# The first segment of a two-layer memory attention + GeGLU kernel in two units of 256 queries, with joined exponentials and a new instruction order

## The chip, the cores and the metric

The kernel runs on one core of one Trainium2 chip. TensorE (PE) multiplies, with its weight loads (PEld) running beside it; VectorE (DVE), ScalarE (ACT) and GpSimd (POOL) do the rest on chip; SyncE (SP) issues DMAs, ScalarE's queue a few more. The metric is device microseconds of one launch.

## The reference

The input x is 2048 tokens by 512. Two equal layers run one after the other, each `x + A(layernorm(x))` and then `x + B(layernorm(x))`, with the same weights in both layers.

- A has 32 heads of width 16 and cuts the tokens into 4 segments of 512, taken in order. In a segment each head does causal softmax attention among the segment's own 512 tokens (`a_dot`), and reads a memory M, z that holds the segments before it: `a_mem = phi(q) M / (phi(q) z + 1e-6)`, with `phi(t) = t + 1 if t > 0 else exp(t)`. The outputs are mixed, `g * a_mem + (1 - g) * a_dot` with `g = sigmoid(beta)` for each head, then `M += phi(k)^T v`, `z += sum phi(k)`. The result goes through `wo`.
- B is `(gelu(x w_gate) * (x w_up)) w_down` with inner width 1792.

Segment 0 of either layer has an empty memory, and no segment needs a later one: the work is causal in segments and, inside one, in tokens.

## The kernel before, in words

**Units.** Tokens lie in tiles of 128; a segment is four tiles (`TPS`). There are eight segment-layers k (`NK`), k = 0 to 3 in the first layer and 4 to 7 in the second, each with an attention object (`Att`, L612 on) and an FFN object (`Ffn`). Everything of one k is for 512 queries at once.

**The order** is written by a planner inside `order()`: it keeps a clock for each engine with a set price for each kind of instruction, a list of PE items (a "due" number and a condition for readiness), and always emits the ready item that is due first. The result is a fixed program; nothing is decided on the chip. Every engine takes its instructions in that order, so a late operand holds up all that stands behind it on its engine. Where the planner sees PE with nothing ready it emits a filler: a product of a tile of ones that nobody reads (L349 before the data arrive, later from the main loop through `product`, L471 and L476, and in the PE transposes of a norm, L584).

**PE modes.** A dense product (`dense`, `product`) is a matmul of 128 rows by 128 columns of weights with 512 columns streamed (L476, "whole"). When a flush is near, the same product is emitted as four matmuls, each on 32 columns of the array (L471, "columns"). Scores use four row tiles (L938), flushes four column tiles (L954).

**Attention.** q and k are produced by block b of 8 heads (128 columns), `par` picks the even or odd heads of a block. Scores of a block and parity come in rounds of 256 streamed columns for four heads each (`FULL`, `round_of`); a ninth round per block, `PAIRED`, holds the 64-wide diagonal halves of both parities, whose left halves use a masked copy of k (`kx`, made by `masked_copies` on DVE, POOL or ACT). `score` emits two rounds at once into four PSUM banks, as two pairs; each pair has one exponential on ACT (L1396, 128 x 1024). POOL then masks the diagonal parts in the probability slots (`mask`, L1343; `mask_half`, L1348; `mask_both` on DVE, L1353). A flush (`flush_item`) multiplies the probabilities of one block and parity with v (`vaug`, with a column for the denominator; the halves in `vz` come by a DMA on SP, L701), and DVE turns, divides and turns back into `aT` (L971 to L989), adding the memory part `amT`.

**FFN.** `wo` products are added to x (L1027), `Norm` takes statistics (L514, L522), POOL makes the scale (L527, L532), DVE or POOL makes `xn` (L544), which PE (L586) or a DMA transposes. `gate` products are evicted and put through gelu in batches (L1151) or directly (L1068, L1054); `up` products are multiplied in (L1092); `down` products are added to x. ACT changes its function table between exponentials and gelu.

**Borrowed space.** q, k, `kx` of k = 0 lie in the space of `wd_sb` and its v in that of `gel_sb`; so the `w_down` loads wait until segment 0 is done (`load_late`), and FFN 0 comes after all of segment 0's attention.

**The start.** x tiles 0 to 3 and beta (copied to 128 partitions by its DMA, L315) come first; ACT makes two of the tile statistics and two exponentials of beta (L1202, L1203), then evicts the first transposes (L599).

```python
fill = FILL if self.key in BY_PE else 0
ops = [(Clocks.MM[512] / 2, whole(lambda: nc.tensor.matmul(
    ps()[:, half:L], lhsT=warm[:], rhs=wide[:, 0:2, :], start=True, stop=True)))] * fill
...
if bank is not None:
    if streams:
        ps = Psum()
        ps.bank = bank
        product(ps(), warm[:], wide)
        ck.on_pe(Clocks.MM[512])
```

Of the kernel before, what the change touches and what calls it, by code (L numbers as in the profile page):

```python
# [41 lines left out]
FULL = [[(0, 64, 256, 0)], [(1, 192, 64, 0), (0, 320, 192, 64)], [(1, 256, 256, 0)], [(3, 448, 64, 0), (2, 320, 192, 64)]]  # L42
DIAG = [1, 1, 0, 2]
# [4 lines left out]
def round_of(t):  # L48

    b, i = divmod(t, ROUNDS)  # L50
    if i == SHARED:
        return b, (0, 1), PAIRED, None
    par = int(i > SHARED)
    return b, (par,), FULL[i - par * (SHARED + 1)], DIAG[i - par * (SHARED + 1)]


BY_PE = {("xnTf", 0), ("xnTf", 1), ("xnTf", NK - 1)}
BANKS = 8
PT_SLOTS = 10
SETS = 3  # L60

# [3 lines left out]
FILL = 2  # L65
# [4 lines left out]
    flush_wait=31.348, piece_slack=5.108, kb_slack=25.115, mem_slack=-15.103, margin=2.314, qk_due=0.572,  # L70
    e_q=-1.218, e_k=1.714, exp_slack=-25.107, e_slack=9.023, phi_slack=17.383, gelu_slack=6.274,
    act_evict=8.464, first_evict=0.965, gate_step=0.061, up_due=-0.553, up_step=0.062, down_due=2.078,
    down_step=0.526, upd_due=0.786, kb_act=6.552, vz_slack=-10.454, x_dve=-0.565, v0_due=-1.4, x1_at=-45.234,
    x2_at=18.289, x3_at=24.819, x3_load=-3.83, direct=4, gelu_tiles=4, look=1.769, lag=0.5, wv_at=8.591,
    xn_pool=7.037, kb_pool=5.303, cut_pool=1.107, at_pool=10.661, pe_turns=2, gate_due=0.765, shun=0.534,
    col_gap=3.33, hold=8, early=4.123, starve=0.308, near=-1.576, cap=4, soon=9.685, columns=0)
# [15 lines left out]
class Engine:  # L92
# [24 lines left out]
    def serve(self, now):  # L117

        self.jobs = [j for j in self.jobs if not j[4]]
        jobs = [j for j in self.jobs if not self.only or j[3] in (None, self.only)]  # L120
        if not jobs:
            return False
        start = max(self.free, min(j[0] for j in jobs) + self.LATENCY)
        if start > now:
            return False
        held = self.rival is not None and self.rival.port > start + 0.25
        job = min((j for j in jobs if j[0] + self.LATENCY <= start + 0.03), key=lambda j: j[0] + j[1] + (
            self.shun if held and isinstance(j[2][0][0], Port) else 0.0))
# [23 lines left out]
        return True  # L152


class Clocks:
# [36 lines left out]
    def serve(self):  # L192

        again = True
        while again:
# [4 lines left out]
            for w in list(self.waiting):  # L200
                if w[0]():
                    self.waiting.remove(w)
                    w[1]()
                    again = True
            first = min(self.engines, key=lambda e: max(e.free, min((j[0] for j in e.jobs), default=1e9)))
            again |= first.serve(self.pe) or any(e.serve(self.pe) for e in self.engines)
# [79 lines left out]
def order(pol, nc, cst, seg, wrk, psp, A_x, A_wq, A_wk, A_wv, A_wo, A_beta, B_x, B_w_gate, B_w_up, B_w_down, out):  # L286
# [15 lines left out]
    beta_bc = cst.tile([P, H], BF16, name="beta_bc")  # L302
# [12 lines left out]
    nc.scalar.dma_start(out=beta_bc[:], in_=A_beta.partition_broadcast(P))  # L315
# [7 lines left out]
    for kt in range(KT):  # L323
        pieces.append((32.0 + 1.2 * kt, 128, lambda kt=kt: load(w_att["o"][:, kt, :], w_view(A_wo)[:, kt, :])))
    for n, (sb, w) in enumerate(((wg_sb, B_w_gate), (wu_sb, B_w_up))):
        for kt in range(KT):
            for h in range(2):
                c = slice(FF * h // 2, FF * (h + 1) // 2)
                pieces.append((37.0 + 1.6 * (8 * n + 2 * kt + h), 224, lambda sb=sb, w=w, kt=kt, c=c: load(
                    sb[:, kt, c], w_view(w)[:, kt, c])))  # L330
    late_pieces = []
# [19 lines left out]
    keep_warm(WARM, 0)  # L351

# [13 lines left out]
    kx0 = wd_sb[:, 2 * KT:FT, :].rearrange("p f l -> p (f l)").rearrange("p (b t c) -> p b t c", b=KT, c=3 * C)  # L366
# [15 lines left out]
    vaugs.append(gel_sb[:].rearrange("p f l -> p (f l)")[:, 0:VALUES])  # L382
# [11 lines left out]
    def later_constants():  # L394
# [5 lines left out]
        for n, va in enumerate(vaugs[-1:] + vaugs[:-1]):  # L400
            ck.dve.post(10.5 + pol.col_gap * n, URGENT if n < 1 else NORMAL,
# [50 lines left out]
    def evict(ps, dst, src, told, slack=NORMAL):  # L452
# [8 lines left out]
        ck.dve.post(ck.made(), slack, (0.673, lambda: nc.vector.tensor_copy(out=dst(), in_=src()), end), taken=taken)  # L461
        ck.act.post(ck.made(), slack + first, (0.602, lambda: nc.scalar.activation(
# [26 lines left out]
    def dense(ps, pairs):  # L489
        n = len(pairs)  # L490
        return [(Clocks.MM[512], lambda i=i, l=l, r=r: product(ps()[:], l(), r(), i == 0, i == n - 1))
                for i, (l, r) in enumerate(pairs)]
# [8 lines left out]
    class Norm:  # L501
        def __init__(self, key, tt0, tag, slack, free):
            self.key, self.tt0, self.tag, self.slack, self.free = key, tt0, tag, slack, free
            self.mv, self.n, self.left = None, 0, TPS
# [4 lines left out]
        def stats(self, j, ready):  # L509
# [6 lines left out]
            def told(t):  # L516
                self.n += 1
                if self.n == TPS:
                    self.scales(t)
# [4 lines left out]
        def scales(self, ready):  # L524
            def first():
                self.ve = wrk.tile([P, TPS, 1], F32, tag="lnve", name="ve")
                nc.gpsimd.tensor_scalar(out=self.ve[:], in0=self.mv[:, :, 1:2], scalar1=EPS_LN, scalar2=None,  # L527
                                        op0=ALU.add)

            def second():  # L530
                self.rs = self.small("rs", 1)
                nc.gpsimd.tensor_tensor(out=self.rs[:], in0=self.ve[:], in1=mhalf[:], op=ALU.pow)  # L532

            ck.pool.post(ready, URGENT, (0.25, first, None),
                         (1.05, second, lambda t: ck.when(self.free, lambda: self.start(max(t, ck.pe)))))

        def start(self, ready):
            self.xnT = seg.tile([P, KT, L], BF16, tag=self.tag, bufs=1, name="xnT")
            for j in range(TPS):
# [35 lines left out]
        def turn_item(self, j, xn, t, landed):  # L575
# [7 lines left out]
            fill = FILL if self.key in BY_PE else 0  # L583
# [26 lines left out]
    class Att:  # L610
        def __init__(self, k):
            self.k, self.s, self.tt0 = k, k % NSEG, TPS * (k % NSEG)  # L612
            self.norm = Norm(("xnTa", k), self.tt0, f"xnTa{k % 2}", URGENT if k == 1 else NORMAL, lambda: k < 2 or ("qkv", k - 2) in ev)
            self.vaug = vaugs[(k - 1) % SETS if k else SETS]
            self.phiq = self.phik = None
            self.n_v, self.n_vz = 0, 0
# [8 lines left out]
        def add_items(self):  # L625
            k, s = self.k, self.s

            def storage():
                return k <= SETS or (("scores", k - SETS) in ev and self.phi_done(k - SETS))

            def first():
                if k:
                    self.q, self.kf = (seg.tile([P, KT, L], BF16, tag=f"{n}{k % SETS}", bufs=1, name=n)
                                       for n in ("q", "kf"))
                    self.kx = kxs[k % 2]
                else:
                    self.q, self.kf = (wd_sb[:, KT * i:KT * (i + 1), :] for i in range(2))
                    self.kx = kx0
# [20 lines left out]
            def k_done(b, ps, at=None):  # L659
# [4 lines left out]
                def told(t):  # L664
                    ev["k", k, b] = t
                    ck.at(t, lambda: ck.when(lambda: k <= 2 or ("scores", k - 2) in ev, copies))
# [858 lines left out]
```

## Time and profile before

| what | value |
|---|---|
| median of 3 runs | 545.62 us (545.53 to 546.54) |
| profiled execution, its own time | 545.75 us |
| span from first to last instruction | 544.0 us |
| granted TensorE clock, mean | 0.999 |
| end of the last matmul | 540.9 us; its result is then added to x (L1027) and stored |
| exponentials, L1396 | 288 of 1025 ns |
| diagonal masks on POOL, L1343 | 192 of 571 ns on average |

The span is that of the instructions; the time of the execution has 1.75 us more around it. Busy times are sums of one engine and overlap with those of the others. For PE, a matmul's shown duration is longer than its share of the array, as the next one begins while it drains; what a stream of matmuls costs is read from start to start.

### The profile page before, as it was taken

To read this page: it belongs to the slowest core of one execution; us is meant where nothing else is said; L and a number is where in the kernel's file an instruction comes from. 1 tells how busy PE (TensorE), PEld (TensorE's weight loads), DVE (VectorE), ACT (ScalarE), POOL (GpSimd) and SP (SyncE) were. 2 spreads that over 40 slices of the span, in tenths; PEclk is the share of its full clock that TensorE was granted. 3 is DMA by queue.
4 is the path that set the end of the run, shared out by engine and by line. 5 is a ranking of instruction groups with operands and counts; after the bars stand their busy time and mean duration, and the time that the engine had idled before them with its cause. 6 is when DMAs were issued, how large, how long until landed. Compare 5 with 4: busy or idle time off the path is not lost.

```text
span 544.0 us, 21276 instructions
## 1 busy us (share of the span) xinstructions
PE 531.3 (98%) x9273; PEld 276.3 (51%) x9334; DVE 443.7 (82%) x816; ACT 434.7 (80%) x540; POOL 305.5 (56%) x359
## 2 busy tenths in 40 slices
PE   8999999999999999999999999999999999999997
PEld 4454555454545444554545555545465456555444
DVE  6998999799988999779987998889586797786342
ACT  5999989988898989989899798996879977920330
POOL 4898786369746788339993468716753265300000
PEclk9999999999999999999999999999999999999999
DMA  8406511610331123310312250221320114100001
GB/s 249 117 13 192 118 20 13 176 33 22 45 56 21 26 40 58 44 40 7 41 32 49 33 72 3 41 32 23 78 52 3 22 21 82 24 3 22 19 0 40
DMA packets 64926, 26.95 MB, mean 50 GB/s; under 512 B 49216, under 2 KB 64832, under 8 KB 64832
## 3 DMA queue, kind: packets, MB, share of 16 engines
q1 hardware_dynamic: 64400, 25.31, 22.6%
q8 instruction: 73, 1.20, 0.9%
q10 hardware_dynamic: 432, 0.27, 0.2%
q14 instruction: 21, 0.17, 0.1%
HBM read 9.71 MB, written 2.10 MB: 22 GB/s over the span
## 4 chain that ended last, share of the span: by engine, by line
PE 88%; DVE 7%; DMA 2%; issue 2%; ACT 0%; ACTq 0%; SPq 0%; DVEq 0%
PE ps L476 46%; PE ps L471 26%; PE ps L938 8%; PE ps L954 7%; DVE st L514 1%; DVE x_sb L1027 1%; DMA beta_bc<-in_A_beta_dram 1%; DVE byq L971 1%; PE ps L586 1%; DVE phiq L745 1%; PE ps L584 1%; DMA phik<-e 0%; DMA amT<-am 0%; DVE xn L544 0%; DVE e L764 0%
## 5 line engine op out<-in xcount | busy, mean ns | idle before, releaser
L1396 ACT ACTIVATE pt<-ps 128x1024 bf16<-128x1024 f32 x288 | 278.9, 1025 | 44.6 <-PE ps L938 41.1
L1343 POOL TENSOR_SCALAR_AFFINE_SELECT pt<-pt 128x256 bf16<-128x256 bf16 (+1 forms) x192 | 107.0, 571 | 118.0 <-ACT pt L1396 112.0
L1092 DVE TENSOR_TENSOR gel_sb<-gel_sb,ps 128x512 bf16<-128x512 bf16 x112 | 75.3, 682 | 33.9 <-PE ps L476 25.0
L476 PE MATMUL ps<-xnT,wu_sb 128*128 128x512 bf16 x287 | 66.8, 379 | 1.4 <-issue 1.1
L476 PE MATMUL ps<-xnT,wg_sb 128*128 128x512 bf16 x261 | 62.6, 379 | 0.9 <-issue 0.5
L764 POOL TENSOR_SCALAR e<-e 128x512 bf16<-128x512 bf16 x37 | 57.9, 1565 | 1.8 <-ACT e L741 0.7
L971 DVE STREAM_TRANSPOSE byq<-ps 128x512 f32<-128x512 f32 x64 | 45.0, 706 | 16.5 <-PE ps L954 15.9
L476 PE MATMUL ps<-wd_sb,gel_sb 128*128 128x512 bf16 (+1 forms) x293 | 56.8, 340 | 1.3 <-issue 1.0
L1348 POOL TENSOR_SCALAR_AFFINE_SELECT pt<-pt 64x1024 bf16<-64x1024 bf16 x40 | 47.8, 1196 | 15.0 <-ACT pt L1396 13.7
L1027 DVE TENSOR_TENSOR x_sb<-x_sb,ps 128x512 bf16<-128x512 bf16 (+1 forms) x68 | 42.8, 640 | 16.3 <-PE ps L476 14.7
L471 PE MATMUL ps<-wd_sb,gel_sb 128*32 128x512 bf16 (+1 forms) x792 | 47.1, 378 | 0.3 <-issue 0.3
L476 PEld LDWEIGHTS <-wu_sb 128*128 128x128 bf16 x301 | 28.2, 98 | 33.8 <-issue 0.7
L471 PE MATMUL ps<-xnT,wg_sb 128*32 128x512 bf16 x700 | 42.4, 380 | 0.0
L514 DVE BATCH_NORM_STATS2 st<-x_sb 128x6 f32<-128x512 bf16 x60 | 40.4, 674 | 0.4 <-DMA x_sb<-in_A_x_dram 0.3
L476 PEld LDWEIGHTS <-wg_sb 128*128 128x128 bf16 x273 | 25.3, 98 | 28.8 <-issue 0.2
L476 PEld LDWEIGHTS <-gel_sb 128*128 128x128 bf16 x306 | 28.3, 98 | 22.7 <-issue 1.1
L954 PE MATMUL ps<-pt,vaug 128*32 128x256 bf16 (+2 forms) x1344 | 34.6, 238 | 0.0
L417 POOL TENSOR_SCALAR kx<-kf,masks 128x512 bf16<-128x512 bf16 x20 | 33.5, 1678 | 1.2
L471 PE MATMUL ps<-xnT,wu_sb 128*32 128x512 bf16 x588 | 34.1, 379 | 0.0
L1151 ACT ACTIVATE gel_sb<-gel_sb 128x2048 bf16<-128x2048 bf16 (+1 forms) x21 | 33.2, 1643 | 0.0
L544 DVE TENSOR_SCALAR xn<-x_sb,mv,rs 128x512 bf16<-128x512 bf16 x58 | 31.3, 592 | 2.2 <-POOL rs L532 1.9
L954 PEld LDWEIGHTS <-vaug 128*32 128x32 bf16 x1344 | 27.8, 97 | 10.4 <-issue 2.2
(147 smaller groups left out, 883.6 us busy)
## 6 DMA issues: line engine op xcount, KB each, us to landing
vz<-vaug SPq DMA_DIRECT2D x14, 136.0 KB, 2.9
wg_sb<-in_B_w_gate_dram SPq DMA_DIRECT2D x8, 224.0 KB, 4.6
wu_sb<-in_B_w_up_dram SPq DMA_DIRECT2D x8, 224.0 KB, 4.3
wd_sb<-in_B_w_down_dram SPq DMA_DIRECT2D x7, 256.0 KB, 4.2
x_sb<-in_A_x_dram SPq DMA_DIRECT2D x3, 512.0 KB, 7.3
out_dram<-x_sb SPq DMA_DIRECT2D x12, 128.0 KB, 1.8
xnT<-xn SPq DMA_TRANSPOSE x40, 2.5
wk_sb<-in_A_wk_dram SPq DMA_DIRECT2D x2, 256.0 KB, 6.0
```

Of the source, the lines that this page charges most:

```text
L471: nc.tensor.matmul(out[r], lhsT=lhsT[:, r], rhs=rhs, start=start, stop=stop, tile_position=(0, 32 * c))
L476: nc.tensor.matmul(out, lhsT=lhsT, rhs=rhs, start=start, stop=stop)
L514: nc.vector.bn_stats(out=self.st6[:, 0, :], in_=x_sb[:, self.tt0 + j, :])
L764: lambda eng: eng.tensor_scalar(out=e[0][:], in0=e[0][:], scalar1=1.0, scalar2=None, op0=ALU.min), summed)
L938: nc.tensor.matmul(ps_all[:, bank, o + c0:o + c0 + n], lhsT=lhsT, rhs=self.q[rows, b, q0:q0 + n], start=True, stop=True, tile_position=(32 ...
L954: nc.tensor.matmul(ps()[32 * j:32 * j + 32, q0:q0 + n], lhsT=va[:, ki * VW + g:ki * VW + g + 32], rhs=pt_all[:, places[i], j, c0:c0 + n], ...
L971: nc.vector.transpose(out=self.byq[:, par, :, :].rearrange("p a c -> p (a c)"), in_=ps()[:])
L1027: ck.dve.post(ck.made(), slack, (0.15 + 0.00104 * (c1 - c0), lambda: nc.vector.tensor_tensor(out=xt, in0=xt, in1=ps()[:, 0:c1 - c0], op=AL ...
L1092: ck.dve.post(ck.made(), NORMAL, (0.683, lambda: nc.vector.tensor_tensor(out=g, in0=g, in1=ps()[:], op=ALU.mult), lambda t: (ps.read(t), e ...
L1343: nc.gpsimd.affine_select(out=view, in_=view, pattern=[[0, 4], [0, n], [1, C]], compare_op=ALU.is_ge, fill=0.0, base=C, channel_multiplier=-1)
L1348: nc.gpsimd.affine_select(out=view, in_=view, pattern=[[0, 4 * TPS], [1, C]], compare_op=ALU.is_ge, fill=0.0, base=0, channel_multiplier=-1)
L1396: nc.scalar.activation(out=pt_all[:, s0:s0 + 2, 2 * p:2 * p + 2, :].rearrange("p r h c -> p h r c"), in_=ps_all[:, pair[0]:pair[1] + 1, :] ...
```

## The change

1. Segment 0 of the first layer becomes two units of 256 queries, u = -1 and u = 0. Scores of its blocks come in another list of rounds (`rounds_of`), two blocks share a paired round, flushes take the unit's queries only (24 or 16 matmuls in place of 40), and each unit has an FFN of its own with two tiles and 256-column products. FFN norms make their scales for two tiles at a time.
2. q, k, `kx` and v of k = 0 get buffers like every other k; the `w_down` loads follow the other weight loads directly, all of which are issued earlier.
3. beta comes as a row of one partition, and one small matmul with ones spreads it over the partitions; the two exponentials of beta stand behind the first evictions on ACT.
4. Equal masks of two rounds become one instruction on POOL; the two exponentials of a double round become one of 128 x 2048 where its four banks are adjacent (`join`).
5. Probability slots are taken from the free ones instead of in a ring; a `wo` product may be begun with three of its four blocks, a first `gate` product with half its tokens.
6. The policy numbers of the planner are others, so the order of all instructions is new. The last norm's transposes get no fillers.

```diff
-FULL = [[(0, 64, 256, 0)], [(1, 192, 64, 0), (0, 320, 192, 64)], [(1, 256, 256, 0)], [(3, 448, 64, 0), (2, 320, 192, 64)]]
-DIAG = [1, 1, 0, 2]
+FULL = [[(1, 192, 64, 0), (0, 64, 192, 64)], [(0, 256, 256, 0)], [(1, 256, 256, 0)], [(3, 448, 64, 0), (2, 320, 192, 64)]]
+DIAG = [2, 0, 0, 2]
+ORDER = [[(1, 2, 0, 3), (1, 0, 3, 2)], [(1, 0, 3, 2), (0, 3, 1, 2)]]
...
+    for u in (-1, 0):
+        for b0 in (0, 2):
+            pair = Round((0, 1), [(b0 + i // 2, ki, P * ki, C, C * i) for i, ki in enumerate(2 * [2 * u + 2, 2 * u + 3])],
+                         None, [(u, b0 + i, par) for i in range(2) for par in range(2)])
+            n = len(rounds)
+            for i in range(4):
+                for m in ((0,) if u < 0 else (1, 2, 3)):
+                    add(u, b0 + i // 2, i % 2, m)
+            rounds.insert(n + (2 if u < 0 else 3), pair)
...
-BY_PE = {("xnTf", 0), ("xnTf", 1), ("xnTf", NK - 1)}
+BY_PE = {("xnTf", -1), ("xnTf", 0), ("xnTf", 1), ("xnTf", NK - 1)}
+UNITS = [(-1, 0, 2), (0, 2, 2)] + [(k, 0, TPS) for k in range(1, NK)]
...
-    nc.scalar.dma_start(out=beta_bc[:], in_=A_beta.partition_broadcast(P))
+    nc.scalar.dma_start(out=beta_row[:], in_=A_beta.partition_broadcast(1))
...
-        late_pieces.append((94.0 + 2.0 * h, 256, lambda r=r: load(
+        pieces.append((pol.wo_at + 2.4 + pol.w_gap * (16 + 1.14 * h), 256, lambda r=r: load(
...
     keep_warm(WARM, 0)
+    beta_ps = ps_all[:, BANKS - 1, 0:H]
+    nc.tensor.matmul(beta_ps, lhsT=warm[0:1, :], rhs=beta_row[:], start=True, stop=True)
...
-                self.q, self.kf = (wd_sb[:, KT * i:KT * (i + 1), :] for i in range(2))
-                self.kx = kx0
...
-            fill = FILL if self.key in BY_PE else 0
+            fill = pol.fill if self.key in BY_PE and self.key[1] < NK - 1 else 0
...
-    def dense(ps, pairs):
+    def dense(ps, pairs, w=L):
...
+    def mask(slot, n, rounds):
+        view = pt_all[:, slot:slot + rounds, :, :].rearrange("p s u c -> p (s u) c")[:, :, 0:C * n].rearrange(
+            "p u (t c) -> p u t c", c=C)
+        nc.gpsimd.affine_select(out=view, in_=view, pattern=[[0, 4 * rounds], [0, n], [1, C]], compare_op=ALU.is_ge,
                                 fill=0.0, base=C, channel_multiplier=-1)
...
+        joined = pol.join > (now[0][0] > 0) and pairs[1][0] == pairs[0][1] + 1
+        for p, got in enumerate([pairs[0] + pairs[1]] if joined else pairs):
...
+            def exp(h0=2 * p, got=got):
                 nc.scalar.activation(
+                    out=pt_all[:, s0:s0 + 2, h0:h0 + len(got), :].rearrange("p r h c -> p h r c"),
+                    in_=ps_all[:, got[0]:got[-1] + 1, :].rearrange("p h (r c) -> p h r c", r=2), func=ACT.Exp, scale=SCALE)
```

More of the change, by code (lines that the diff above doesn't have):

```diff
@@ L199, in serve @@
                 again = True
[L200 to L206, printed above, removed]
+            if self.waiting:
+                for w in list(self.waiting):
+                    if w[0]():
+                        self.waiting.remove(w)
+                        w[1]()
+                        again = True
+            best = None
+            for e in self.engines:
+                if e.jobs:
+                    t = e.next_start()
+                    if t is not None and t <= self.pe and (best is None or t < best):
+                        best, first = t, e
+            if best is not None:
+                first.serve(best)
+            elif not again:
+                return
     def dma_load(self, t, kb):
@@ L1303, in tight @@
     def tight():
-        return any(slot_free[slot_of(k, t)] is None for k, t in streams[2:4])
+        return len(free_slots()) < 2
     def rounds_ready(n):
@@ L1310, in rounds_ready @@
                 return False
-        return len(streams) >= n and all(slot_free[slot_of(k, t)] is not None for k, t in streams[:n])
+        return len(streams) >= n and len(free_slots()) > 0
     def rounds_now(idle=False):
@@ L1336, in open_item @@
         items.remove(it)
+        if it.kind == "half":
+            return it
         it.ps.bank = bank
@@ L1445, in order @@
                 got = [it for it in items if it.after in ev and it.ready() and (
-                    it.kind != "flush" or not streams or tight() or it.posted < late or ck.mode == "columns")]
+                    it.kind != "flush" or not streams or tight() or it.posted < (late if it.flush < KT - 1 else ck.pe - pol.last_wait) or ck.mode == "columns")]
                 if got:
```

431 lines of the change are left out of this document (246 added, 185 removed).

## Prediction

> **What bounds the kernel.** I read the page's busy shares first, then PE's own waits, then the groups that PE issues, and last the chain of waits.
>
> ```profile
> span 544.0 us, 21276 instructions
> PE 531.3 (98%) x9273; PEld 276.3 (51%) x9334; DVE 443.7 (82%) x816; ACT 434.7 (80%) x540; POOL 305.5 (56%) x359
> PE 88%; DVE 7%; DMA 2%; issue 2%; ACT 0%; ACTq 0%; SPq 0%; DVEq 0%
> ```
>
> PE is busy 531 of 544 us, and the chain that ends last is PE for 88%. The view of waits, for PE alone, confirms that this is work and not waiting:
>
> ```profile
> PE ps L476 <- issue: 4.3, 27, 0.2
> PE ps L349 <- DVE warm L340: 1.1, 1, 1.1
> PE ps L596 <- DVE xn L544: 1.0, 2, 0.7
> PE ps L586 <- DVE byq L971: 0.3, 1, 0.3
> ```
>
> After the start no single wait is over 0.3 us. ("issue" here is mostly matmul records missing from the trace.) So the time is the sum of what PE issues, plus the start and the tail, and an edit counts where it changes that sum or brings back a wait. But not all that PE issues is needed. Groups by form, fillers alone:
>
> ```profile
> L476 PE MATMUL ps<-warm 128*128 128x512 bf16 x19 | 5.4, 381 | 0.0
> L584 PE MATMUL ps<-warm 128*128 128x256 bf16 x24 | 4.6, 274 | 0.0
> L471 PE MATMUL ps<-warm 128*32 128x512 bf16 x48 | 2.9, 379 | 0.0
> ```
>
> Durations overlap, so I take prices from start to start in the timeline of PE:
>
> ```profile
> 466.93 0.40 PE L938 MATMUL ps<-q,kx 32*128 32x256 bf16 x12
> 467.26 1.68 PE L476 MATMUL ps<-xnT,wg_sb 128*128 128x512 bf16 x7
> 474.87 12.26 PE L471 MATMUL ps<-xnT,wu_sb 128*32 128x512 bf16 x224
> 486.96 3.63 PE L471 MATMUL ps<-wo_sb,aT 128*32 128x512 bf16 x64
> ```
>
> From 474.87 to 486.96 stand 224 matmuls on column tiles, four to a product: 12.09 / 56 = **0.216 us** for 512 columns. Dense whole products begin 0.216 us apart too, 256-column ones 0.109. A score block takes 467.26 - 466.93 = 0.33 us; its 256 streamed columns are 0.107 of it, so its two changes of tile mode cost about 0.11 each.
>
> **The ledger of PE.** I counted every matmul in both programs' orders, by kind, with columns in streams of four tiles counted once.
> - Needed work is the same: 2048 score and 2560 flush matmuls in either, the same dense columns; some 482 us of streaming at 0.216 for 512 columns in both. There are 144 score blocks in both; the changes of tile mode go from 301 to 299, -0.2 us.
> - Fillers after the start, before: 19 + 48/4 = 31 of 0.216 and 24 of 0.109, 9.3 us. After: 4 + 48/4 = 16 of 0.216 and 16 of 0.109, 5.2 us. **-4.1 us.**
> - Halves of 256 columns: 280 products in place of 140, each pair 2 x 0.109 - 0.216 = 0.002 dearer: +0.3.
> - The tiny denominators (`zcols`, 8 columns): 64 whole and 128 tiled before, 18 and 312 after. Starts are 25 ns apart whole and 8 tiled: 2.6 to 2.9 us, +0.3. The one beta matmul is nothing beside 15 fillers of the start.
>
> **The start.** The chain in order of time:
>
> ```profile
> 1.71 5.38 DMA beta_bc<-in_A_beta_dram
> 7.11 0.23 ACT macc L1202
> 7.34 0.12 ACT tmp_e L1203
> 7.46 0.98 ACT xnT L599 x2
> ```
>
> ACT waits for beta until 7.09 and evicts the first transposes only then, though the first of those end near 7.0. After, ACT evicts first. The new beta matmul stands ahead of the transposes on PE, so a late row would hold up all of PE; but the 15 fillers run to 5.9 and xn to 6.6, and a row in one partition is less than the 128 KB x tiles, which land in 2.7 to 3.0: 1.71 + 3.0 = 4.7 (estimate). The bounds are 0 (the row as late as the old DMA) and -0.4 (7.46 to 7.05). In addition PE stood from 10.23 to 10.56 before its first score; now ten dense products fill that place while ACT makes the first `kx`: -0.3 at best. I take **-0.6**, nearer the far end, since both waits are seen in rows.
>
> **The other edits, which lie beside PE.**
> - Joined exponentials: 75 of the 144 double rounds. The trace has no 128 x 2048 from PSUM. Bounds: two separate ones, 2.05, and 1025 + 1024 x (1025 - 612)/512 = 1.85 from the copies of 512 at 612 ns; a 128 x 2048 gelu from SBUF takes 1.93. I take 1.87, nearest to that slope: -13.5 us of ACT. Four more table loads of 1.28 give +5.1; ACT makes 24 v evictions in place of 10, and with its other rows I sum +3 for ACT in all. It stays near 438 of 531: hidden under PE. If joining saves nothing, ACT is at 451, still under.
> - Masks on POOL: 192 of 107.9 us become 59 of some 1.27 (from 483 at 256 and 745 at 512, another 262 for each 256 more) and 10 of 0.745: 82. With fewer `kx` and minima, POOL falls by some 41 us; a mask begins with the later exponential of its pair, which the flush may wait for. DVE takes over `kx` (24 instead of 10) and minima (18 for 11) and loses v evictions: +3 of 444. Both remain under PE.
> - ACT from 8.7 to the 12th double round is the tightest stretch: 18 exponentials at 0.94 (pairs take 1.94 in the timeline, with the overlap), 2 joined, 24 evictions at 0.55 to 0.58, four `kx` pairs at 1.15 and small ones: 41.3 us, so it gets there at 49.9. PE's order (49.5 by the ledger) gets there at the same moment. The same sum for the kernel before agrees with its trace within 0.3 us at 49.8. So no slack and no loss; a bound of +1.
> - Weights: wo, gate, up, down, 6 MB, are issued from about 13 us; in the trace nine loads (2 MB) from 44.0 landed by 52, some 258 GB/s: all there by 41. The first gate is at 46.8, the first `down` at 62.6. On SP the first `vz` is behind wo and two gate loads, about 1 MB or 4 us; the first flush, near 27, has some 3 us to spare.
> - The tail, from 478 on, is dense work in both; the wait for the last norm was filled with 8 of the 24 small fillers and is now filled with `down` products.
>
> **Sum.** -4.1 - 0.2 + 0.3 + 0.3 - 0.6 = -4.3 on 545.75 of the profiled execution (544.0 of span and 1.75 around it): 541.4. Waits of PE that no filler hides I take as before: the page shows about 1 us of them at the start and another 0.3, and the new order has as many handoffs; +0.2. **541.6 us**; the profiled execution is 0.13 above the median, which I leave. Its own range is 540.0 to 544.4.
>
> [...] The new order emits much more dense work in column mode: 185 us against 147. In this trace that is free, as 56 such products took 12.09 us, 0.216 each as whole ones do. [...]
>
> **The rivals.**
> 1. *Fillers come back as waits.* A filler stands where PE had nothing ready. Taking it out gains only if work came into its place; else PE idles there and 4.1 us return: 545.7. For it: two chains `wo` to norm to transposes are now in segment 0 instead of one. Against: in the new order q and k products stand in those gaps, 7 and 8 us long, and the chain (additions, statistics, scale, xn at the rows' durations) is about 5.2. Chance 0.11. That weights come too late for the earlier first FFN, so that it doesn't do what it is made for, also ends between 543 and 546; chance 0.03.
> 2. *Slower: the joined exponential holds four PSUM banks.* Two separate ones give back two banks after 0.94, the joined one gives back all four after 1.87, so a score or product behind it on PE can come 0.93 later, and so can the masks. Half of the 8 banks are taken. Each of the 75 that PE feels costs up to 0.93; 5 of them eat the gain, 8 give 541.6 + 7.5 = 549. Against: PE's waits name ACT nowhere, and dense work stands between scores. Chance 0.12.
> [...]
>
> **The numbers.** Forecast 0.73, return of waits 0.11, late weights 0.03, banks 0.12, tiles 0.01. What a measurement can tell from no change here is about 0.2%, 1.1 us: 544.5 to 546.7. Faster: 0.73 and half the late weights, 0.74; same: 0.11 and the other half, 0.12; slower: 0.13 and rounding, 0.14. The range reaches from 540.0 through the return of waits to 546.3 and leaves out the banks and tiles.
>
> **What would show it.** In the new profile: 32 fewer fillers' worth (about 68 filler matmuls after the start against 91); the first score near 12 with dense products ahead of it and ACT's first eviction near 7.05; the last matmul near 536.7; PE's waits still without ACT or POOL in any amount over 1 us; joined exponentials near 1.87; ACT and DVE below 85% of the span. The forecast is wrong if the view of PE's waits shows several us behind ACT `pt`, `vz` or `xn`, most likely before 90 us, or if the joined exponential is over 2.05.

## The result and the profile after

The changed kernel takes **553.14 us** (median of four: 551.54 to 554.44) against 545.99 (four: 545.53 to 546.54) on the same chip: ratio 1.0129, 95% interval 1.0093 to 1.0165. It is slower by some 7 us, where 541.6 was forecast. The profiled execution is the shortest of the four, 551.54 us with a span of 549.8; it is 5.8 us above that of before.

The page of the kernel after, its first lines and the shares of the chain of waits:

```profile
span 549.8 us, 23348 instructions
PE 531.9 (97%) x10437; PEld 292.8 (53%) x10487; DVE 447.9 (81%) x861; ACT 440.9 (80%) x485; POOL 263.8 (48%) x242
PE 81%; DVE 13%; issue 3%; ACT 3%; DMA 1%; POOL 0%; DVEq 0%; ACTq 0%
```

PE's busy time looks unchanged (531.9 for 531.3). The chain tells more: DVE ends 13% of it in place of 7%. PE's waits by line and releaser (us in total, times, longest):

```profile
PE ps L526 <- issue: 4.3, 27, 0.2
PE ps L521 <- issue: 2.3, 2, 1.7
PE ps L521 <- DVE x_sb L1088: 1.3, 1, 1.3
PE ps L521 <- DVE byq L1023: 1.1, 2, 0.9
PE ps L526 <- DVE gel_sb L1180: 0.8, 2, 0.5
PE ps L521 <- ACT pt L1507: 0.6, 2, 0.3
```

In the same view of before no single wait after the start was over 0.3. Now there are single ones of 1.3 and 0.9 behind DVE's evictions, and two in L521 that end at "issue", that is at nothing the profile shows: 2.3 us, the longest 1.7. The 27 small "issue" waits in L526 are matmul records missing from the trace, as before (after's trace has 10,437 matmuls for 10,487 weight loads).

I set every matmul of the program against its record in the trace and took off what the ledger of the prediction allows for it (0.216 for 512 columns, 0.11 for a change of tile mode, and so on). What is left over is waiting, and it is read as a sum that grows along the span. (Counted so, from start to start, a single wait is up to 0.4 us longer than in the view, where the shown duration of the matmul ahead of it covers a part.)

| stretch | waits before | waits after | more |
|---|---|---|---|
| to 21 us (start) | 3.45 | 3.08 | -0.4 |
| 21 to 58 | 0.44 | 3.63 | +3.2 |
| 58 to 81 | 0.41 | 1.69 | +1.3 |
| 81 to 141 | 0.92 | 2.68 | +1.8 |
| 141 to 222 | 0.03 | 2.40 | +2.4 |
| 222 to the end | 1.09 | 2.36 | +1.3 |
| PE's ledger | 534.4 | 530.7 | -3.7 |

The sum, -3.7 - 0.4 + 10.0 = 5.9, is the 5.8 of the profile within rounding. So PE does issue 3.7 us less, as forecast, and gives back ten in waits. Thirteen waits of 0.3 to 2.0 us make up 9.3 of after's 12.8 from 21 us on; two such in before make 1.1. They are of two kinds.

**PE without instructions.** In PE's timeline (start, duration, matmuls) two waits of 2.9 us together stand in the middle of products whose operands had been used a moment before; this is the longer one:

```profile
35.84 1.03 PE L521 MATMUL ps<-wv_sb,xnT 128*32 128x512 bf16 x14
38.56 0.39 PE L521 MATMUL ps<-wv_sb,xnT 128*32 128x512 bf16 x2 [1.69 <-issue]
```

The page's part on queues has a queue of instructions:

```profile
q8 instruction: 82, 1.34, 1.0%
```

82 packets of 16 KB: with 20,976 instructions on PE that is one for each 256. (Before: 73 for 18,670.) The trace's DMA records date each. Half of the 82 packets start between 0.4 us before and 0.8 us after PE enters the block ahead, nine in ten within 1.3 us of it. A packet takes about 1.0 us, and where PE stood for one it went on 1.25 to 1.6 us after the packet's end. The packets of 30.84 and 36.10 us came 3.8 and 2.9 us late.

Both stops stand at the end of a block: the matmuls after them are 128 apart in the program, which with their weight loads is 256 instructions. The sums of the two: in the second, PE enters at 33.19, has 3.35 us of work in the block, and waits 2.91 + 1.16 + 1.31 - 3.35 = 2.03; measured 2.02. In the first, 3.8 + 0.98 + 1.37 - 5.24 = 0.91; measured 0.91. (The 1.31 and 1.37 are read from the stops themselves, so the sums show only that the work ahead of a stop ends with the block.)

What stands beside the late packets is in the windows of two microseconds (busy time and instructions by engine; last, the granted clock, the DMA share and GB/s):

```profile
34.00:36.00 2.00, 2.00 (x101) 1.36 (x98) 1.63 (x4) 1.75 (x4) 1.91 (x2) 1.00 1.11 350
36.00:38.00 2.00, 0.87 (x18) 0.21 (x7) 1.89 (x6) 2.00 (x3) 1.92 (x2) 1.00 0.42 134
```

The 16 DMA engines are full until about 36.5 (share 1.11 at 350 GB/s in the first window): gate, up, x and down loads are issued without a pause from 18.8 to 32.7 us, and the seven `down` loads take 6.5 us from issue to landing (median) against 4.2 before. The second packet starts, at 36.10, as they drain; with the loads spread neither packet is over 0.75 us late (experiment 1). Before has one such stop too, at 398 us, with 0.64 us by the ledger: the packet started at 395.67, took 1.00, and PE went on 1.4 later. Its view of waits has it as

```profile
PE ps L471 <- issue: 0.3, 1, 0.3
```

**PE without a bank.** This is the wait at 210 us, DVE and PE in their timeline:

```profile
209.34 1.46 DVE L797 SCALAR_TENSOR_TENSOR phiq<-q,e 128x512 bf16<-128x512 bf16 x1
210.73 0.68 DVE L566 BATCH_NORM_STATS2 st<-x_sb 128x6 f32<-128x512 bf16 x1
211.55 0.66 DVE L1088 TENSOR_TENSOR x_sb<-x_sb,ps 128x512 bf16<-128x512 bf16 x1
212.25 0.62 PE L521 MATMUL ps<-xnT,wg_sb 128*32 128x256 bf16 x16 [1.29 <-DVE x_sb L1088]
```

The gate product has its operands; the bank it was given still holds a `down` product that DVE adds to x only at 211.55, behind a phi and the statistics. Those near 64 us (1.2 in sum, behind `gel_sb`) and at 131 (1.1, where even a filler waits for `byq` to leave its bank) are like it; at 103 (0.5) PE waits for a joined exponential itself. One at 195 (0.4) is for an operand, `aT`. The order foresaw them: where nothing is ready **and no bank is free**, the planner moves its own clock on by 0.05 us and writes nothing, and its record of these steps holds 16 of them before 480 us in before (0.8 us) and 169 after (8.45 us), at 33, 61 to 63, 102, 130, 134, 194, 210 us. In all 169 no bank is free; in 117 four adjoining banks are held up to one and the same moment, as an exponential of 128 x 2048 holds them. These are planned, not measured, times, but PE's measured waits stand near most of those places.

### The profile page after: what moved, and what is told of

It is laid out like the page before. It is cut to its first block, busy times and chain, and to the rows that moved or that the text cites. A ratio compares the mean times of both kernels' runs of the same rounds, so it can differ in the third digit from the quotient of the medians.

```text
span 549.8 us, 23348 instructions
## 1 busy us (share of the span) xinstructions
PE 531.9 (97%) x10437; PEld 292.8 (53%) x10487; DVE 447.9 (81%) x861; ACT 440.9 (80%) x485; POOL 263.8 (48%) x242
## 4 chain that ended last, share of the span: by engine, by line
PE 81%; DVE 13%; issue 3%; ACT 3%; DMA 1%; POOL 0%; DVEq 0%; ACTq 0%
PE ps L526 36%; PE ps L521 30%; PE ps L987 7%; PE ps L1008 6%; ACT pt L1507 2%; DVE st L566 2%; DVE x_sb L1088 1%; DVE phiq L797 1%; DVE byq L1023 1%; DVE xn L601 1%; DVE ab L1031 1%; PE ps L643 1%; DVE gel_sb L511 1%; DMA x_sb<-in_A_x_dram 1%; DVE gel_sb L1180 1%
## 5 line engine op out<-in xcount | busy, mean ns | idle before, releaser
L1507 ACT ACTIVATE pt<-ps 128x1024 bf16<-128x1024 f32 (+1 forms) x213 | 274.2, 1327 | 35.4 <-PE ps L987 31.4
L1436 POOL TENSOR_SCALAR_AFFINE_SELECT pt<-pt 128x1024 bf16<-128x1024 bf16 (+1 forms) x69 | 79.2, 1148 | 100.3 <-ACT pt L1507 99.9
L1180 DVE TENSOR_TENSOR gel_sb<-gel_sb,ps 128x512 bf16<-128x512 bf16 (+1 forms) x126 | 76.4, 623 | 32.5 <-PE ps L526 26.2
L526 PE MATMUL ps<-xnT,wu_sb 128*128 128x512 bf16 (+1 forms) x386 | 78.5, 355 | 2.1 <-DVE gel_sb L1180 0.8
L521 PE MATMUL ps<-wd_sb,gel_sb 128*32 128x512 bf16 (+1 forms) x1108 | 61.6, 367 | 0.0
L526 PEld LDWEIGHTS <-wu_sb 128*128 128x128 bf16 x395 | 37.7, 98 | 37.8 <-issue 1.7
L1023 DVE STREAM_TRANSPOSE byq<-ps 128x512 f32<-128x512 f32 (+1 forms) x72 | 45.9, 643 | 14.7 <-PE ps L1008 14.6
L526 PE MATMUL ps<-xnT,wg_sb 128*128 128x512 bf16 (+1 forms) x259 | 54.6, 347 | 2.4 <-issue 1.3
L521 PE MATMUL ps<-xnT,wg_sb 128*32 128x512 bf16 (+1 forms) x1024 | 52.1, 343 | 1.3 <-DVE x_sb L1088 1.3
L1041 POOL TENSOR_TENSOR aT<-aT,amT 128x512 bf16<-128x512 bf16 x16 | 18.8, 1178 | 52.5 <-DVE aT L1038 40.6
L526 PE MATMUL ps<-wd_sb,gel_sb 128*128 128x512 bf16 (+1 forms) x219 | 41.8, 341 | 1.3 <-issue 1.3
L521 PEld LDWEIGHTS <-gel_sb 128*32 128x32 bf16 x1108 | 28.6, 97 | 22.4 <-issue 0.6
L1008 PEld LDWEIGHTS <-vaug 128*32 128x32 bf16 x1536 | 31.6, 97 | 13.5 <-issue 6.7
L526 PEld LDWEIGHTS <-wg_sb 128*128 128x128 bf16 x276 | 25.4, 98 | 23.8 <-issue 2.3
L987 PE MATMUL ps<-q,kx 32*128 32x64 bf16 (+2 forms) x1280 | 35.8, 217 | 0.3
L521 PEld LDWEIGHTS <-wg_sb 128*32 128x32 bf16 x1024 | 25.6, 97 | 16.5 <-issue 2.5
```

The source lines that it names most:

```text
L521: nc.tensor.matmul(out[r], lhsT=lhsT[:, r], rhs=rhs, start=start, stop=stop, tile_position=(0, 32 * c))
L526: nc.tensor.matmul(out, lhsT=lhsT, rhs=rhs, start=start, stop=stop)
L987: nc.tensor.matmul(ps_all[:, bank, o + c0:o + c0 + n], lhsT=lhsT, rhs=self.q[rows, b, q0:q0 + n], start=True, stop=True, tile_position=(32 ...
L1008: nc.tensor.matmul(ps()[32 * j:32 * j + 32, q0:q0 + n], lhsT=va[:, ki * VW + g:ki * VW + g + 32], rhs=pt_all[:, slot, j, c0:c0 + n], start ...
L1023: nc.vector.transpose(out=self.byq[:, par, some, :].rearrange("p a c -> p (a c)"), in_=ps()[:, cols])
L1180: ck.dve.post(ck.made(), NORMAL, (0.15 + 0.533 * share, lambda: nc.vector.tensor_tensor(out=g, in0=g, in1=ps()[:, 0:w], op=ALU.mult), lamb ...
```

## The experiments

All times are medians, each beside runs of before on the same chip (545.7 to 546.1). "The order is kept" means that every other instruction of every engine stands where it stood.

**1. Weight loads spread (order kept but on SP).**

```diff
-    pieces.append((pol.wo_at + 2.4 + pol.w_gap * (8 * n + 2 * kt + h), 224, ...
+    pieces.append(((pol.wo_at + 2.4, 44.0)[n] + (pol.w_gap, 0.8)[n] * (2 * kt + h), 224, ...
-    pieces.append((pol.wo_at + 2.4 + pol.w_gap * (16 + 1.14 * h), 256, ...
+    pieces.append((52.2 + 0.8 * h, 256, ...
```

> The kernel after with only the order of SP's loads changed: the eight up loads stand behind the first transposing DMA of phik and the seven down loads behind the second, so that 1.8 MB in place of 5.4 MB are issued from 18.8 us on. All other engines have the order of the kernel after. Theory (PE's own instructions come late): in the trace of after PE's 16 KB instruction packets that started at 30.84 and 36.10 us came 204 and 217 matmuls after the fetch before was due, where others come about 100 after, and PE stood 0.91 + 2.02 us, and 0.25 beside, in the middle of products with all their operands there. Without the crowd these stalls go: about -3.0 us, 548.5 for the profiled execution of 551.5; packets start at about 100 again. Rival (the stalls are operands or banks late, the packets are innocent): the stalls stay, within 0.5 us of after.

550.10 us (550.0 to 550.4), ratio 1.0072 [1.0059, 1.0084]: 3.0 under the median of after. The packets start at 27.80 and 32.07, 0.75 us late and not late, and both stops are gone: at 41 us the waits sum to 4.07 in place of 6.30. The profiled execution gained only 1.3 (550.22 for 551.54), since two stops of the same kind came up at 100.0 (0.53) and 103.6 (0.91), where the blocks are short, and one of 0.59 behind ACT `pt` at 33.2. The other 1.7 us of the medians is probably the clock, as argued under experiment 4. The theory stands, with less than half of its gain in the profiled execution; its rival is out.

**2. Before, with its loads crowded (order kept but on SP).**

```diff
-    pieces.append((32.0 + 1.2 * kt, 128, ...
+    pieces.append((13.1 + 0.6 * kt, 128, ...
-    pieces.append((37.0 + 1.6 * (8 * n + 2 * kt + h), 224, ...
+    pieces.append((15.5 + 1.05 * (8 * n + 2 * kt + h), 224, ...
```

> The kernel before with only SP's loads moved: wo, gate and up, 4.1 MB, are issued from about 8 us on without a pause, as in after (the down weights can't, their place holds q and k of segment 0). All other engines have the order of before. Theory (crowded loads delay PE's instruction packets): the packets that start at 25.6 and 32.5 us now, 108 and 112 matmuls after their mark, come later by some microseconds, and PE stands between 1 and 3 us in the middle of a product: 547 to 549. With 1.3 MB less in the queue than in after, nearer to 1. Rival (before would bear the crowd, and after's stalls come from its own order): 545.5 to 546, as before.

546.06 us, ratio 0.9998 [0.9988, 1.0007]: the time of the rival. The packet did come later, 27.70 in place of 25.64, 2.4 us after PE entered its block. But that block holds 6.4 us of work, so 2.4 + 1.0 + 1.4 = 4.8 stays hidden. In this run the crowd alone cost nothing: it did not outlast the work of the block.

**3. After without its fillers.**

```diff
-                product(ps(), warm[:], wide)
...
-            ops = [(Clocks.MM[512] / 2, whole(lambda: nc.tensor.matmul(
-                ps()[:, half:L], lhsT=warm[:], rhs=wide[:, 0:2, :], start=True, stop=True)))] * fill
+            ops = [(Clocks.MM[512] / 2, whole(lambda: None))] * fill
```

> The kernel after with its 16 fillers of 512 columns and 16 of 256 left out, in the same order otherwise; the 15 at the start stay. They add up to 5.2 us of PE. Theory (a filler stands where PE has nothing ready, so it covers a wait): the waits come out in its place, and the time falls by less than 1.5 us. Rival (the fillers of this order stand in PE's way, as the sum of the prediction counted those of before): -4 to -5 us.

556.62 us, ratio 1.0193 [1.0176, 1.0209]: 3.5 *over* after, with 5.2 us less to issue. Both theories missed it; the first was nearer. The waits come out, and a second cost with them. PE's waits, then the windows:

```profile
PE ps L986 <- ACT pt L1506: 3.0, 4, 1.8
PE ps L526 <- DVE aT L1040: 1.8, 2, 1.6
```

```profile
132.00:136.00 4.00, 1.49 (x54) 0.79 (x39) 3.90 (x7) 4.00 (x5) 3.92 (x3) 0.94 0.49 101
136.00:140.00 4.00, 3.11 (x26) 1.01 (x27) 3.86 (x8) 3.35 (x4) 3.89 (x3) 0.50 0.53 104
140.00:144.00 4.00, 4.00 (x43) 1.54 (x45) 3.13 (x8) 2.38 (x4) 3.24 (x5) 0.71 0.00 0
```

PE stands for 1.8 and 1.6 us close together, is busy 1.49 of 4 us, and the granted clock falls to 0.50 for 6.8 us. A third cost lies in the view's "issue":

```profile
PE ps L521 <- issue: 3.8, 5, 2.0
```

By the ledger eight waits of 0.3 us or more, 6.9 us in sum, stand at the end of an instruction block, with a packet that ended 1.3 to 1.6 us before; in after it was two of 2.9 us. My estimate from these times is that PE, with less to do in a block, reaches its end before the next one is there. Fillers are no waste here: without them the waits came out, the mean clock was 0.994 in place of 1.000 (profiled executions) and, as far as this run shows, the packets had less time.

**4. Each joined exponential issued as two (order otherwise kept).**

```diff
+                for h in range(0, len(got), 2):
                     nc.scalar.activation(
-                    out=pt_all[:, s0:s0 + 2, h0:h0 + len(got), :]..., in_=ps_all[:, got[0]:got[-1] + 1, :]...
+                        out=pt_all[:, s0:s0 + 2, h0 + h:h0 + h + 2, :]..., in_=ps_all[:, got[h]:got[h + 1] + 1, :]...
```

> The kernel after with each joined exponential issued as two of 128 x 1024 one behind the other; the order of every engine is kept. ACT gets 75 x (2 x 1.026 - 1.88) = 12.9 us more, and the first two of the four banks come free about 0.85 us earlier. Theory (the long hold has already cost what it costs when the order was laid down: with four banks held, the order gives PE's next product the bank of an eviction on DVE or ACT, and PE waits there): no gain, between 0 and +3 us. Rival (PE waits for the joined exponential itself, for a bank or for the masks behind it): the earlier banks give 2 to 5 us back.

552.72 us (551.99 to 554.56), ratio 1.0124 [1.0104, 1.0143]: no gain, as the theory had it: at a clock of 0.999 or more its executions take 552.0 to 552.9, those of after 551.5 and 552.0. PE's order already gives the product the bank of an eviction, and earlier banks of the scores are of no use to it.

Its profiled execution, 554.56, shows what the longer executions of after (554.3 and 554.4, mean clock 0.997, against 551.5 and 552.0 at 1.000 and 0.999) probably hold. The second stop at 36 us is 2.2 us here and not 1.7:

```profile
36.00:38.00 2.00, 0.11 (x2) 0.00 (x0) 1.90 (x6) 1.54 (x2) 1.92 (x2) 1.00 0.37 116
38.00:40.00 2.00, 1.65 (x21) 0.78 (x24) 1.41 (x3) 1.22 (x3) 0.67 (x2) 0.72 0.04 10
40.00:42.00 2.00, 2.00 (x24) 0.95 (x20) 0.00 (x0) 0.39 (x1) 0.00 (x0) 0.50 0.00 0
```

The clock is 0.50 from 38.9 to 42.3, and in the window from 40 to 42 us PE, busy throughout, shows 24 matmuls where after shows 44. After had no trace of its longer executions, so for them this is argued. For it speaks that with the stop removed (experiment 1) all five executions lie within 0.4 us at clock 1.000. The clock fell after the stop of 2.2 us here, and did not after the one of 1.7 in after or one of 2.0 in experiment 3 (at 36.6 us).

**5 to 8. Parts undone, with a new search of the policy numbers.** A change of parts changes the whole order, so its numbers were searched anew by the planner's own estimate, which is a weak tool.

Number 5 has segment 0 whole (units, rounds and flushes as for k > 0), 50 exponentials joined and spread loads; number 6 keeps the halves, with 46 joined; number 7 keeps them with none joined; number 8 is number 5 with the load times of after.

```diff
-UNITS = [(-1, 0, 2), (0, 2, 2)] + [(k, 0, TPS) for k in range(1, NK)]
+UNITS = [(k, 0, TPS) for k in range(NK)]
...
-        joined = pol.join > (now[0][0] > 0) and pairs[1][0] == pairs[0][1] + 1
+        joined = len(streams) not in SINGLE and pairs[1][0] == pairs[0][1] + 1
```

> The kernel after with the halved segment 0 undone: segment 0 runs as one unit of 512 queries like the other seven, with their rounds; beta as a row, merged masks, joined exponentials (now 50 of them, 188 single) stay. The policy numbers were searched anew for this order, and SP's loads are spread as in before. In this order the fillers and the planner's own idle steps before 480 us add up to 35 x 0.216 + 2.3 = 9.9 us; in after they are 5.2 + 8.45 = 13.7, in before 9.3 + 0.8 = 10.1. Theory (the two halves leave the order with more moments in which all eight banks are held, and PE idles there; joined exponentials are bearable without them): 545 to 546, at or under before, with no wait of PE over 1 us after the start but issue. Rival (the joined exponentials alone carry the loss): stays at 548 to 550, as after with spread loads.

554.91 us, ratio 1.0162 [1.0149, 1.0175]. Neither theory: it is worse than both said. Its waits:

```profile
PE ps L523 <- DMA phik<-e: 1.8, 2, 1.0
PE ps L523 <- DVE gel_sb L513: 1.7, 1, 1.7
PE ps L1010 <- DVE x_sb L1090: 1.7, 1, 1.7
PE ps L523 <- issue: 1.6, 1, 1.6
```

The search had found an order that is short only by the planner's prices: a transposing DMA and two evictions come later than it believes.

> The kernel after with its halves, loads spread as in the first experiment, 29 of the 75 joined exponentials single again (46 joined, 196 single, chosen by a search together with the policy numbers). Fillers and the planner's idle steps: 5.4 + 6.7 = 12.1 us, 1.5 under after. Theory (what the order itself leaves idle is what the chip shows): 548 to 549, that is 1.5 to 2 under after with spread loads (550.1). Rival (the planner's idle steps mean nothing on the chip): within 0.7 us of 550.1.

549.93 us, ratio 1.0077 [1.0062, 1.0093]: within 0.2 of experiment 1, so the planned 1.5 us did not come. PE's stops for instructions are 3.7 us here against 1.8 there (one of 1.72 at 52.8, beside up loads that were issued from 45 us), which could hide it. It settles nothing.

> The kernel after with its halves, no exponential joined (288 single), policy numbers searched anew, loads spread. Fillers and idle steps: 43 x 0.216 + 5.5 = 14.8 us. Theory (halves are the cost, with or without joining): 549 to 551. Rival (joining is the cost, it holds four banks at a time): without it the time falls to that of before, 546 or less.

553.04 us, ratio 1.0126 [1.0111, 1.0141]. Without any joined exponential it is no faster; the rival's 546 is out for this order, but with 2.7 us of stops for instructions and a weak search it does not clear the joining either.

> The first kernel of this call (segment 0 whole) with only SP's loads changed, to the times of after: wo, gate, up and down, 5.4 MB, from about 8 to 33 us without a pause. All other engines keep their order. Theory (PE's instruction packets queue behind the loads): the packets that should start between 25 and 40 us come over 200 matmuls after the fetch before was due, PE stands in the middle of products, and the time is 1.5 to 5 us above the first kernel. Rival (only after's own order is hurt): within 0.5 us of the first kernel.

552.20 us, ratio 1.0114 [1.0101, 1.0127]: 2.7 *under* number 5, the wrong way for the theory as I had put it, and right for its mechanism. In number 5 the spreading itself put nine loads between 66.3 and 71.1 us beside a short block. PE there:

```profile
75.70 0.29 PE L1010 MATMUL ps<-pt,vz 128*32 128x64 bf16 x16
77.64 0.40 PE L523 MATMUL ps<-xnT,wq_sb 128*32 128x512 bf16 x4 [1.65 <-issue]
```

The packet started 2.72 us late, at 75.21: 2.72 + 1.01 + 1.42 - 3.33 us of work = 1.82, measured 1.83. In number 8 those loads go out early, where a packet is 1.6 late beside 6.5 us of work, and the stop is away. The spans of the two profiled executions, 551.9 and 550.3 us, differ by about that stop. The other 1.1 us of the medians may be the clock: the other executions of number 5 ran at 0.996 and 0.997, those of number 8 at 1.000. So not "when the loads are early" but "what block they fall upon".

**9. Before, with neighbouring exponentials joined (order kept).** Only the first banks come free later than the order was laid down for: after 1.88 us in place of 1.03.

```diff
+            def exp(p=p, exps=exps):
+                if p == 0 and joined:
+                    HELD.append((ck.act, lambda: exps(0, 1), set(pairs[0]), partner[1]))
+                elif p and HELD and HELD[0][3] is partner[1]:
+                    HELD.clear()
+                    exps(0, 2)
```

> The kernel before with the order of every engine kept; only where a double round's two exponentials stand next to each other on ACT and their four banks adjoin, they are issued as one: 53 joined, 182 single. The first two banks of these come free 0.85 us later than the order was laid down for, ACT saves 53 x 0.17 = 9 us. Theory (a joined exponential costs by the banks it holds, where PE's next scores or products were given the first two): PE waits for ACT pt in several places, 2 to 8 us in sum, 548 to 554. Rival (dense work always stands between, the hold isn't felt): 545.5 to 546.3, as before.

**553.10 us**, ratio 1.0131 [1.0117, 1.0145]: 53 joined exponentials cost 7.4 us, with ACT 2 us less busy (432.4 for 434.7). Here ACT's `pt`, which before named nowhere, leads PE's waits:

```profile
PE ps L481 <- ACT pt L1409: 3.0, 6, 0.9
PE ps L476 <- ACT pt L1409: 1.5, 3, 0.7
PE ps L943 <- ACT pt L1409: 0.9, 4, 0.3
```

Thirteen waits, 5.4 us, none over 0.9; waits after the start sum to 10.1 by the ledger against 2.9. In the timeline at 220 us a gate product waits for a bank of one of them:

```profile
219.44 1.88 ACT L1409 ACTIVATE pt<-ps 128x2048 bf16<-128x2048 f32 x1 [0.32 <-DVE am L825]
221.37 0.59 PE L481 MATMUL ps<-xnT,wg_sb 128*128 128x512 bf16 x2 [0.71 <-ACT pt L1409]
```

The theory stands, with a price of 0.14 us for each joined one on average.

**10 and 11. A shorter DVE instruction, in experiment 1's kernel and in before (order kept).**

```diff
-                nc.vector.bn_stats(out=self.st6[:, 0, :], in_=x_sb[:, self.tt0 + j, :])
+                nc.vector.bn_stats(out=self.st6[:, 0, :], in_=x_sb[:, self.tt0 + j, 0:64])
```

> The first experiment (after with spread loads) with one instruction shortened on DVE: the statistics of the norms, but for those of the first tiles, are taken of 64 of the 512 columns, so what is normalised differs. The order of every engine is kept. Some 60 instructions of 676 ns become about 150 ns, 30 us off DVE's 448. Theory (what is left of the loss is PE waiting for evictions that queue on DVE while the other four banks are held by scores): the waits at 131 us (1.1, byq) and 210 us (1.4, x) shrink, and some smaller ones, -1 to -3 us from 550.1. Rival (the order leaves PE idle for another reason than late evictions): within 0.5 us of 550.1.

547.79 us, ratio 1.0032 [1.0021, 1.0044]: 2.3 under experiment 1. The statistics take 216 ns in place of 676. The wait at 210 us is gone:

```profile
207.72 0.21 DVE L566 BATCH_NORM_STATS2 st<-x_sb 128x6 f32<-128x64 bf16 x1
208.34 0.69 DVE L1088 TENSOR_TENSOR x_sb<-x_sb,ps 128x512 bf16<-128x512 bf16 x1 [0.19 <-PE ps L521]
209.11 0.62 PE L521 MATMUL ps<-xnT,wg_sb 128*32 128x256 bf16 x16
```

The one at 131 us, behind `byq`, stayed at 1.1. The two near 62 us, 1.2 in sum behind `gel_sb`, came back as one of 1.2 behind ACT `pt`.

> The kernel before with the same shortened statistics, as the control: its trace shows no wait of PE for DVE over 0.3 us between 35 us and the end, so a faster DVE has nothing to give back. Expected by the theory: within 0.5 us of before. Rival (a shorter DVE helps any order, by less contention or earlier norms): 1 us or more under before.

545.65 us, ratio 0.9995 [0.9986, 1.0004]: nothing, as expected. The shorter statistics pay only in the order in which PE runs out of banks, though DVE is busy 82% in before and 81% in after. Experiments 1 and 10 together take the ratio from 1.0129 to 1.0032, that is three quarters of the loss.

**12. Before with the start of the change alone.**

```diff
+    nc.tensor.matmul(beta_ps, lhsT=warm[0:1, :], rhs=beta_row[:], start=True, stop=True)
...
-    nc.scalar.activation(out=tmp_e, in_=beta_bc[:], func=ACT.Exp)
...
     n0.first_turn(1)
+    nc.scalar.activation(out=tmp_e, in_=beta_ps, func=ACT.Exp)
```

> The kernel before with only the start of the change: beta loaded as a row of one partition and spread by one matmul into PSUM, the two exponentials of it behind ACT's first two evictions. Everything else keeps its order. Theory (ACT's wait for beta to 7.1 us holds up the first evictions): ACT's first eviction at 7.05 in place of 7.46, everything behind it earlier by up to 0.4 us: 545.2 to 545.6, at the edge of what can be told, and the only part of the change that can be had without a new order. Rival (the row is late too, or the wait is taken up before the first score): as before, 545.7.

545.98 us, ratio 1.0000 [0.9991, 1.0009]. ACT evicts at 7.18 where before does at 7.37 and its first score exponential starts 0.16 us earlier (10.83 for 10.99); the rest was lost by the end. No kernel of these beats before.

## Why the prediction was wrong

1. **The failing step is "Waits of PE that no filler hides I take as before", +0.2.** They grew by 10 us. The 3.7 us less that PE issues, the change of start (-0.4 of -0.6), the column tiles (no dearer: in after's timeline 64 such matmuls, 16 products, take from 493.64 to 497.10, 0.216 us each), the joined exponential (1.88 for 1.87) and the shares of ACT and DVE (80 and 81%) came as worked out. (One reading beside the path was wrong: the 13.5 us that joining was to save on ACT were taken from durations that overlap. The busy time of the exponentials fell from 278.9 to 274.2, by 4.7.) A right ledger of work says nothing of gaps.
2. **"Fillers: -4.1 us" counted the wrong thing.** I took 31 + 24 fillers becoming 16 + 16 as work put in their place. But the kernel writes a filler only `if bank is not None`. With no free bank it writes nothing, and the program's order does not show that it stood idle. By its own record, fillers and idle steps went from 9.3 + 0.8 = 10.1 to 5.2 + 8.45 = 13.7: a rise of 3.6, not a fall of 4.1. Rival 1, the return of waits, had the sign, but capped it at what the fillers had been.
3. **Rival 2, four banks held, was the nearer story, and I gave it 0.12.** Its price, up to 0.93 for each that PE feels, 549 in all, is borne out in size by experiment 9: 7.4 us for 53 in an order not made for them. "PE's waits name ACT nowhere, and dense work stands between scores" was read from a kernel whose order frees two banks at a time; the dense work needs banks too. In after, the order was made with joined exponentials, so PE waits less for ACT than for DVE's evictions of the other four: splitting the exponentials gave nothing back, a shorter DVE instruction gave 2.3 us (experiments 4 and 10). That the four held banks are the reason rests on the planner's record, 117 of 169 idle steps; no run shows it alone.
4. **"Weights ... all there by 41" was right and missed the point.** Nothing waited for weights. I priced the loads by who reads them and not by what else uses the DMA engines: PE's own instructions. That is 2.9 us in the profiled execution, and perhaps 1.7 more in the median by the clock, as far as experiments 1 and 4 show. The prediction's view of PE's waits left out the row of 0.3 us that shows such a stop in before.
5. Of the signs I had named, filler matmuls came to 68 as forecast, and the last matmul at 546.7 in place of 536.7 and waits behind DVE in several us, most before 222 us, told against it.
6. No run shows the dearer column tiles that the forecast gives a chance of 0.01 and leaves out of its range. What the runs showed in their place is the 0.216 us of item 1, and a ledger at that price whose sum, 5.9 us, meets the 5.8 of the profile.

What stays open: how the other 7 us or so of new waits (4.2 of them are read above as waits for a bank or an exponential) divide between the joined exponentials, the halved segment and the new policy. Experiments 5 to 8 were to show it and did not, as every newly searched order had faults of its own. An order for the halves with single exponentials that is as good as before's was not found.

## What to carry to other kernels

Before crediting a shorter sum of work, look for the resource that an order needs for filling its gaps (here eight PSUM banks): an instruction that holds four of them twice as long can take away both the work and the filler that would have hidden it (53 of them cost 7.4 us in experiment 9). Fewer fillers may mean worse gaps (32 and 8.45 us of idle steps in after, 55 and 0.8 in before), so count the planner's silent idle steps as well. When loads are moved, ask which instruction block of the busiest engine they will fall upon: one of 3.33 us of work brought a stop of 1.83 in number 5, one of 6.4 none in experiment 2.

## What the runs showed of the hardware

- PE's instructions came over the DMA engines, 256 to a packet of 16 KB (in after 82 packets for 20,976, in before 73 for 18,670), half of after's packets sent between 0.4 us before and 0.8 us after PE entered the block ahead. A packet took about 1.0 us, and where PE stood for one it went on 1.25 to 1.6 us after the packet's end. At the three stops worked out above that show late packets (2.7 to 3.8 us late), the lateness, the packet and the time after it came to 0.9 to 2.0 us more than the work of the block, and PE stood for as long; in experiment 2 they came to 4.8 us beside 6.4 of work, and it did not stand.
- Column tiles and flushes used up a block fastest: 224 matmuls on column tiles took 12.09 us, so 128 of them take 6.9 (estimate), where 128 whole ones at 0.216 take 27.6 (estimate); a flush of 40 matmuls took 0.67 us. The shortest block lasted 1.9 us in after (from 457.6, with two flushes and 8-column products) and 2.9 in before (from 395.2, the one with the stop at 398).
- The granted clock fell to 0.50 after one gap of 2.2 us (experiment 4), and after two of 1.8 and 1.6 close together (experiment 3), for 3.4 and 6.8 us; after one of 1.7 (after) and one of 2.0 (experiment 3) it did not. No run shows what decides.
